# A packed attention with a gated MLP: the second product by seven products instead of eight, and float16 weights parked in DRAM

## The chip, the core and the metric

The kernel runs on one core of a Trainium2 chip. The metric is the time of one execution in device microseconds (us), and less is better. On the core, TensorE (PE in the profile) multiplies matrices into PSUM, a small accumulator memory; VectorE (DVE), ScalarE (ACT) and GpSimd (POOL) do elementwise work; SyncE (SP) only starts DMAs here. Each engine takes its instructions in the order in which the program lists them and waits on semaphores for the others. SBUF is the on-chip memory of 128 partitions in which tiles live; DRAM is the memory that DMAs read and write.

## What is computed

Eight batches of eight heads, 576 tokens and 64 values a head. 32 "packed" rows a head attend to the tokens, then the tokens attend to the packed rows; the result, 4608 tokens of 512 values, goes through an RMS norm and a gated MLP of width 1536.

```python
p_packed = sm_attn(p, k, v)                 # 32 rows a head
out = sm_attn(q, p_packed, p_packed)        # all tokens
x = out, heads side by side                 # 4608 x 512
xn = x / sqrt(mean(x * x) + 1e-06) * rms_g
g = xn @ w_gate                             # 512 -> 1536
val = xn @ w_val
return (g * sigmoid(g) * val) @ w_out       # 1536 -> 512
```

`sm_attn` is a softmax over scaled scores times the values. `q`, `k`, `v`, `p` and the output are float32; the MLP's weights arrive as 64-bit floats, and the kernel turns them into float32 first (`to_f32`, line 484).

## The kernel before

**The arithmetic.** The attention result of a token is its softmax weights over 8 x 32 = 256 packed rows times those rows. So gate and value can be taken straight from the 256 softmax weights, if the packed rows of each batch are first multiplied into `w_gate` and `w_val`. These are the *packed weights* (`packed_weights`, line 1184): per batch six chunks `c` of 256 gate and 256 value columns. The *first product* is then softmax weights (256 deep) times packed weights; its result passes through SiLU and the multiplication of gate and value; the *second product* multiplies the resulting `h` (1536 deep) by `w_out`. Most float32 values are held as a sum of two float16 parts, high and low, and a product is three float16 matmuls into one accumulator: high by high, high by low, low by high.

**The loops.** `mlp` (line 1590) goes over 12 units `u` of 384 tokens, which are three tiles of 128. For each of 12 blocks `ft` of 128 hidden columns it makes gate and value (line 1620: two depths of 128 and three passes, six matmuls of 384 columns each). A batch has 576 tokens, so units 1, 4, 7 and 10 hold tokens of two batches: there every matmul is split into two of 192 columns, since each batch has its own packed weights. `gated` (line 1660) then takes SiLU on ScalarE (line 1671), multiplies on VectorE (line 1674), and splits the result into high (line 1694, ScalarE) and low part (line 1700, VectorE, the difference of a float32 and a float16 tile in SBUF). After the 12 blocks, each of the three tiles runs 36 matmuls of 512 columns against `w_out` (line 1656), and `store` (line 1706) scales the result (line 1712) and sends it out (line 1715).

**Packed weights.** They live in a ring of eight places, six being one batch, so most chunks of batch b+1 can only be made while the unit at the boundary uses up the chunks of batch b (mark `used`). For batches 0 to 3 they are made from float32 weights (line 1212), for batches 4 to 7 (`PW16_FROM`) in three float16 passes (line 1223). In between `weights16` (line 1231) turns the weights in `wgv` in place into two float16 parts, through VectorE (line 1238), ScalarE (line 1240) and GpSimd (line 1242). `pw_evict` brings the packed weights from PSUM into the ring as high and low parts (`split`, lines 457 and 459).

**Everything else** runs beside this: `keysets` and `stage1` make the packed rows of the next batches, `query` (line 1326) loads and transposes the queries of a unit and `attention` (line 1394) makes its softmax weights; `query` may start when the first product of unit u - 2 has been issued (mark `po`). Many of the transposes are DMAs.

**The order.** All engines' instructions are written out by a small planner in the file (`Plan`, line 88). Each piece of work is a generator that yields its engine and an estimated cost. The planner picks the next piece by the earliest estimated start within a window (`CHOICE`) and a rank for each kind of work (`RANK`, `LATER`); `Room`s are buffers that are handed round, among them four PSUM banks `pm` that first product, second product and packed weights share, and two output buffers `o`. Strings such as `H_LO` say for each block which engine does an operation ("A" ScalarE, "D" VectorE, "P" GpSimd). The planner's times fix the order within each engine's queue, those of SP included; what runs when is then settled by semaphores.

## Time and profile before

| quantity | value |
|---|---|
| time, median of 3 runs | 779.63 us (779.62, 779.63, 781.18) |
| span of the profiled execution | 778.5 us; the fastest run is 1.1 us longer than it, which lies around the span |
| TensorE's granted clock, mean | 0.991 |
| bytes moved by DMA | 82.21 MB, 135509 packets |

The profile is one execution. Its page gives each engine's busy time, the chain of work that ended last and the costliest groups of instructions; further views answer for a stretch of time or a line. A group reads: line, engine, operation, written tile <- read tiles, shapes, count, then busy us and mean ns of one, then the idle time of the engine before it and who ended that. A row in order of time reads: start, duration, engine, line, operation, tiles, count, and in brackets idle time before it. Matmuls are pipelined, so a matmul's own duration is longer than the distance to the next one. PEld are weight loads, which overlap matmuls.

### The profile page before, as it was taken

The page shows a single profiled execution, that of the slowest core. Times are in us where ns is not written, and L with a number is a line of the kernel's source. Part 1 is how long each engine was busy: PE and PEld are TensorE (multiplying, and loading weights), DVE is VectorE, ACT ScalarE, POOL GpSimd, SP SyncE. Part 2 cuts the span into 40 slices and gives each one's busy share as a digit, 9 for nine tenths or more (in the row PEclk, how much of TensorE's full clock was granted, in tenths as well). Part 3 has the DMA queues.
Part 4 walks back from the last instruction along what each step waited for, and adds up shares of the span by engine and source line. Part 5 has one row for each costly group of instructions (what it writes and reads, how often), then busy time and mean ns, then how long its engine had stood idle before and what let it go on. Part 6 is the DMA issues. An engine that isn't in the chain of part 4 may idle for free.

```text
span 778.5 us, 18543 instructions
## 1 busy us (share of the span) xinstructions
PE 738.2 (95%) x7778; PEld 436.5 (56%) x7778; DVE 507.1 (65%) x1095; ACT 473.4 (61%) x910; POOL 84.3 (11%) x95
## 2 busy tenths in 40 slices
PE   8767899999999989999989999999999999999998
PEld 6533564686445455576544456468455455685553
DVE  1698889685585687589688559458468355472341
ACT  3679987676586668587678558447357265271230
POOL 1545121000000012013311000000000000000000
PEclk9899999999999999999999999999999999999999
DMA  9999700565366436636436653723213212300001
GB/s 255 386 278 259 232 16 21 99 114 143 72 114 145 86 66 153 140 66 139 107 85 116 104 136 63 160 66 62 55 49 63 68 35 64 92 19 26 27 1 41
DMA packets 135509, 82.21 MB, mean 106 GB/s; under 512 B 98433, under 2 KB 123009, under 8 KB 135425
## 3 DMA queue, kind: packets, MB, share of 16 engines
q1 hardware_dynamic: 135424, 81.02, 43.8%
q8 instruction: 61, 1.00, 0.5%
q14 instruction: 24, 0.19, 0.1%
HBM read 47.97 MB, written 9.44 MB: 74 GB/s over the span
## 4 chain that ended last, share of the span: by engine, by line
PE 72%; DVE 12%; DMA 6%; ACT 5%; issue 2%; SPq 1%; POOL 1%; DVEq 0%; ACTq 0%; POOLq 0%
PE pm_3x L1656 9%; PE pm_1x L1656 8%; PE pm_2x L1656 8%; PE pm_2x L1620 7%; PE pm_0x L1620 7%; PE pm_1x L1620 7%; PE pm_3x L1620 7%; PE pm_0x L1656 6%; DMA ring<-in_moe_w_gate_dram 2%; PE quad L1421 1%; PE quad L1058 1%; DVE ring L459 1%; PE quad L1498 1%; DMA big_5x<-in_v_dram 1%; DVE wgv L499 1%
## 5 line engine op out<-in xcount | busy, mean ns | idle before, releaser
L1620 PEld LDWEIGHTS <-ring 128*128 128x128 f16 x2304 | 204.8, 98 | 107.3 <-issue 36.6
L1656 PEld LDWEIGHTS <-hall 128*128 128x128 f16 x1296 | 123.6, 98 | 146.4 <-issue 8.4
L1656 PE MATMUL pm_2x<-wo,hall 128*128 128x512 f16 x360 | 81.9, 379 | 0.0
L1656 PE MATMUL pm_3x<-wo,hall 128*128 128x512 f16 x360 | 81.7, 379 | 0.0
L1656 PE MATMUL pm_1x<-wo,hall 128*128 128x512 f16 x324 | 74.8, 379 | 0.0
L1694 ACT CAST hall<-t_1x 128x384 f16<-128x384 f32 x71 | 36.3, 511 | 34.7 <-DVE t_1x L1674 34.6
L1656 PE MATMUL pm_0x<-wo,hall 128*128 128x512 f16 x252 | 56.9, 379 | 0.0
L1620 PE MATMUL pm_2x<-aTu_0x,ring 128*128 128x384 f16 (+1 forms) x312 | 45.8, 289 | 1.8 <-DVE ring L459 1.4
L1694 ACT CAST hall<-t_0x 128x384 f16<-128x384 f32 x70 | 35.5, 508 | 18.8 <-DVE t_0x L1674 18.7
L1700 DVE TENSOR_TENSOR hall<-t_1x,hall 128x384 f16<-128x384 f32 x70 | 39.7, 567 | 10.7 <-ACT hall L1694 9.1
L1620 PE MATMUL pm_2x<-aTu_1x,ring 128*128 128x192 f16 (+1 forms) x312 | 43.7, 283 | 1.3 <-ACT t_0x L1671 0.9
L1620 PE MATMUL pm_3x<-aTu_0x,ring 128*128 128x192 f16 (+1 forms) x312 | 42.4, 280 | 2.6 <-DVE ring L459 2.6
L1620 PE MATMUL pm_1x<-aTu_1x,ring 128*128 128x192 f16 (+1 forms) x300 | 42.3, 284 | 2.2 <-DVE o_1x L1712 1.2
L1700 DVE TENSOR_TENSOR hall<-t_0x,hall 128x384 f16<-128x384 f32 x70 | 40.0, 571 | 6.6 <-ACT hall L1694 6.4
L1620 PE MATMUL pm_0x<-aTu_1x,ring 128*128 128x192 f16 (+1 forms) x300 | 42.4, 285 | 0.0
L1620 PE MATMUL pm_0x<-aTu_0x,ring 128*128 128x384 f16 (+1 forms) x240 | 37.7, 298 | 2.1 <-ACT t_1x L1671 1.5
L1620 PE MATMUL pm_3x<-aTu_1x,ring 128*128 128x384 f16 (+1 forms) x240 | 36.6, 294 | 2.7 <-ACT t_1x L1671 1.9
L1620 PE MATMUL pm_1x<-aTu_0x,ring 128*128 128x192 f16 (+1 forms) x288 | 39.0, 279 | 0.1
L1532 POOL TENSOR_TENSOR trio_6x<-trio_5x,neghalf 128x3 f32<-128x3 f32 x6 | 5.1, 852 | 232.0 <-DVE trio_5x L1526 232.0
L1242 POOL TENSOR_TENSOR wgv<-o_0x,wgv 128x512 f16<-128x512 f32 x12 | 14.4, 1203 | 107.7 <-ACT wgv L1240 65.0
L1532 POOL TENSOR_TENSOR trio_2x<-trio_1x,neghalf 128x3 f32<-128x3 f32 x6 | 5.1, 856 | 152.1 <-DVE trio_1x L1526 152.0
L1454 ACT ACTIVATE hl_0x<-e_0x 128x768 f16<-128x768 f32 x10 | 8.4, 843 | 20.9 <-DVE e_0x L1445 15.6
(917 smaller groups left out, 1348.7 us busy)
## 6 DMA issues: line engine op xcount, KB each, us to landing
out_dram<-o_0x SPq DMA_DIRECT2D x18, 256.0 KB, 2.0
out_dram<-o_1x SPq DMA_DIRECT2D x18, 256.0 KB, 2.0
hall<-in_moe_w_out_dram SPq DMA_DIRECT2D x4, 1024.0 KB, 5.4
wo<-in_moe_w_gate_dram SPq DMA_DIRECT2D x3, 1024.0 KB, 15.5
wo<-in_moe_w_val_dram SPq DMA_DIRECT2D x3, 1024.0 KB, 11.5
big_5x<-in_v_dram SPq DMA_DIRECT2D x5, 576.0 KB, 6.7
big_0x<-in_v_dram SPq DMA_DIRECT2D x4, 576.0 KB, 6.6
big_3x<-in_k_dram SPq DMA_DIRECT2D x4, 576.0 KB, 6.5
```

Source lines behind the costliest of these rows:

```text
L459: nc.vector.scalar_tensor_tensor(lo, x, s, hi, ALU.mult, ALU.subtract)
L499: nc.vector.scalar_tensor_tensor(d, d, 3, lo, ALU.logical_shift_left, ALU.bitwise_or)
L1058: nc.tensor.matmul(pp[32 * j : 32 * j + 32, :D], a1T[:, c, 32 * j : 32 * j + 32], vf[:, j, cv, :], start=(c == 0), stop=(c == NCK - 1),)
L1242: nc.gpsimd.tensor_tensor(wgv16[:, c, k, 1], st, wgv16[:, c, k, 0], ALU.subtract)
L1421: nc.tensor.matmul(ps2[o : o + n, i, :, pi, :], qT[:, lq, i, pi, o : o + n], packs[b][3][:, lp, pi, :, :], start=(j == 0), stop=(j == 2),)
L1454: nc.scalar.activation(ehl[:, :, 0, :], e, AF.Copy, scale=2.0**14)
L1498: nc.tensor.matmul(px[o : o + n, j, i, g, :], aT[h, i, la, g, o : o + n], packs[b][2][g][h, lp, :], start=(n3 == 0), stop=(n3 == 2), tile_ ...
L1532: nc.gpsimd.tensor_tensor(ru, var, neghalf.broadcast_to([P, TPU]), ALU.pow)
L1620: nc.tensor.matmul(psi[:, :, o : o + n], pw[:, g, lw, w, f * P : (f + 1) * P], aT[:, :, la, g, o : o + n], start=(j == 0), stop=(j == 5),)
L1656: nc.tensor.matmul(po, hall[:, ft, lh, ts], wo[:, ft, 1 - lw, :], start=(n == 0), stop=(n == 3 * NFT - 1))
L1694: nc.scalar.copy(hall[:, ft, 0, :], t)
L1700: nc.vector.tensor_tensor(hall[:, ft, 1, :], t, hall[:, ft, 0, :], ALU.subtract)
```

## The change

1. From token 768 on (`GROUPS_FROM` = 2 units) the MLP goes by 15 groups `g` of 256 tokens (two tiles) instead of units of 384. The first product makes 2 x 128 hidden columns by 256 tokens in one PSUM bank, in matmuls of 256 columns; where the two tiles are of different batches, or a batch ends inside a tile, in pieces of 128 or 64 (`pieces`). For this the tokens of units 4, 7 and 10 are dealt to the tiles so that only the middle tile holds two batches (`blocks`); loads and stores follow. Attention, queries and keys still go by units of 384.
2. From group 7 on (`SEVEN_FROM`) the second product is done by Strassen's scheme. The 256 tokens by 256 hidden columns of a chunk are a 2 x 2 block matrix, the 256 hidden columns by 512 outputs another. Instead of eight products of 128 x 128 by 256 blocks there are seven, in which one or both factors are sums of blocks (`out_seven`). Four sums on the side of `h` are made by GpSimd for every chunk (`sums`) and split into float16 parts with `h` itself (`halves`): 7 blocks of 128 columns instead of 4. The four sums on the side of `w_out` are made once (`differences`). `collect` adds the seven products up into the two output tiles, with one ScalarE and seven VectorE operations of 256 columns in place of two of 512. Groups 3 to 6 keep the old form in the new tiling (`out_plain`).
3. The float16 weights are ready from batch 2 on (`PW16_FROM` 4 -> 2), so the conversion runs earlier. Each chunk's float16 parts are written once to DRAM (`keep`, 6 x 1 MB); from batch 3 on each chunk is brought back into one of three places of `wgv` before its packed weights are made (`bring`, 30 x 1 MB, at most three chunks ahead). The other three places then hold the sums of `w_out`.
4. The planner's constants, its ranks, the engine strings and some buffers are others; branches that no setting used are gone.

The core of the diff:

```diff
-SLACK = (0.317, 0.223)
-CHOICE = ({'pe': 0.1, 'act': 0.458, 'dve': 0.275, 'pool': 0.298, 'sp': 0.833}, {'pe': 0.0, 'act': 0.417, 'dve': 0.193, 'pool': 0.208, 'sp': 0.274})
+SLACK = (0.175, 0.244)
...
-PW16_FROM = 4
-V16_FROM = 8
+PW16_FROM = 2
...
+GROUPS_FROM = 2
+SEVEN_FROM = 7
+NGT = 256
+AHEAD = 4
+T_HI = "ADADAA"
+T_LO = "DDDPDD"
+G_HI = "AADAAA"
+G_LO = "DDDDDD"
+S_BY = "PPPP"
+S_HI = "AAAAAA"
+S_LO = "DPPDDD"
...
+    tb = wgv[:, :3].rearrange("p c k w f -> p (c k w f)").bitcast(F16)
+    tb = tb.rearrange("p (k c l n) -> p k c l n", k=4, c=NFC, l=2)
+    dram = ctx.enter_context(tc.tile_pool(name="dram", bufs=1, space=bass.MemoryType.DRAM))
+    kept = [dram.tile([P, NKT * 2 * 2 * P], F32, name=f"kept{c}") for c in range(NFC)]
...
+    seven = hall0.rearrange("p (c l k t) -> p c l k t", c=NFC, l=2, k=7)
...
+    aTus = cpool.tile([P, 2 * TPU, 2, 2, P], F16, name="aTus")
+    for i in range(2):
+        plan.rooms[f"aTu{i}"] = [(0.0, aTus[:, TPU * i : TPU * (i + 1)])]
+    plan.rooms["s"] = []
...
+            w16 = wgv16[:, c]
             if b == PW16_FROM:
                 yield ("wgv16", c, NKT - 1)
+            elif b > PW16_FROM:
+                yield ("brought", b, c)
+                w16 = wgv16[:, brought_at(b, c)]
...
+            if k == NKT - 1:
+                plan.add(keep(c), "keep", c)
+    def keep(c):
+        yield LOAD, P * 8192
+        nc.sync.dma_start(kept[c], wgv[:, c].rearrange("p k w f -> p (k w f)"))
+        plan.mark("kept", c)
+    def brought_at(b, c):
+        return 3 + (NFC * (b - PW16_FROM - 1) + c) % 3
+    def bring():
+        for n in range(NFC * (B - PW16_FROM - 1)):
+            b, c = PW16_FROM + 1 + n // NFC, n % NFC
+            if n < 3:
+                yield ("pw16", PW16_FROM, 3 + n)
+                yield ("kept", 3 + n)
+            else:
+                yield ("pw16", *divmod(n - 3 + NFC * (PW16_FROM + 1), NFC))
+            yield ("kept", c)
+            yield LOAD, P * 8192
+            nc.sync.dma_start(wgv[:, brought_at(b, c)].rearrange("p k w f -> p (k w f)"), kept[c])
+            plan.mark("brought", b, c)
+    def differences(c):
+        for i in range(3):
+            yield ("pw16", PW16_FROM, i)
+            yield ("kept", i)
+        yield ("wo_hl", c)
+        room = yield Room("big")
+        r = room[:, : 4 * NGT].rearrange("p (f n x) -> p f n x", f=2, n=2)
+        x = wo[:, 2 * c : 2 * c + 2].rearrange("p f l (n x) -> p l f n x", n=2)
+        yield POOL, pool(4 * NGT)
+        nc.gpsimd.tensor_tensor(r, x[:, 0], x[:, 1], ALU.add)
+        for to, a, b in (((0, 0), (0, 1), (0, 0)), ((0, 1), (1, 1), (0, 1)), ((1, 1), (1, 1), (0, 0)), ((1, 0), (1, 0), (1, 1))):
+            yield POOL, pool(NGT)
+            nc.gpsimd.tensor_tensor(r[:, *to], r[:, *a], r[:, *b], ALU.subtract)
+        rr = r.rearrange("p f n x -> p (f n) x")
+        if T_HI[c] == "A":
+            yield ACT, act(4 * NGT)
+            nc.scalar.copy(tb[:, :, c, 1], rr)
+        else:
+            yield DVE, 0.074 + 0.53e-3 * 4 * NGT
+            nc.vector.tensor_copy(tb[:, :, c, 1], rr)
+        if T_LO[c] == "D":
+            yield DVE, dve(4 * NGT)
+            nc.vector.tensor_tensor(tb[:, :, c, 0], rr, tb[:, :, c, 1], ALU.subtract)
+        else:
+            yield POOL, pool(4 * NGT)
+            nc.gpsimd.tensor_tensor(tb[:, :, c, 0], rr, tb[:, :, c, 1], ALU.subtract)
+        plan.give("big", room)
+        plan.mark("tb", c)
...
+    def blocks(u):
+        (b, r, _, n), *more = parts(u)
+        if not more or u < EARLY:
+            return [(b, 0, TPU, o, n, r) for b, r, o, n in parts(u)]
+        return [
+            (b, 0, 2, 0, n, r), (b, 0, 1, n, P - n, r + 2 * n),
+            (b + 1, 1, TPU, n, P - n, 0), (b + 1, 2, TPU, 0, n, 2 * (P - n)),
+        ]
...
+        ahead = TPU * u // 2 - AHEAD
+        if ahead >= GROUPS_FROM * TPU // 2:
+            yield ("po", ahead, "group")
+        elif u > 1:
+            yield ("po", min(u - 2, GROUPS_FROM - 1))
...
+        yield from by_units()
+        if SEVEN_FROM == GROUPS_FROM * TPU // 2:
+            plan.add(sums_rooms(), "sums")
+        for g in range(GROUPS_FROM * TPU // 2, NU * TPU // 2):
+            yield from group(g)
+    def by_units():
...
+    def pieces(g):
+        at = [tile_parts(*x) for x in group_tiles(g)]
+        if at[0] == at[1]:
+            return [(b, slice(0, 2), o, n) for b, o, n in at[0]]
+        return [(b, slice(i, i + 1), o, n) for i in range(2) for b, o, n in at[i]]
+    def group(g):
+        tiles = group_tiles(g)
+        us = sorted({u for u, _ in tiles})
+        n0 = TPU * (tiles[0][0] % 2) + tiles[0][1]
+        aT = aTus[:, n0 : n0 + 2]
+        later = {x[0] for n in range(2 * g + 2, TPU * NU) for x in tile_parts(*divmod(n, TPU))}
+        done_b = sorted({x[0] for x in pieces(g)} - later)
+        for u in us:
+            yield ("aTu", u)
+        for c in range(NFC):
+            for b in sorted({x[0] for x in pieces(g)}):
+                yield ("pw", b, c)
+            for u in us:
+                yield ("sc", u)
+            pss, done = [], []
+            for w in range(2):
+                ps = yield Room("pm")
+                psi = ps.rearrange("p (f i t) -> p f i t", f=2, i=2)
+                yield PE, pe(NGT, 12)
+                for f in range(2):
+                    for b, i, o, n in pieces(g):
+                        pw = ring[:, slot_of(b, c)]
+                        j = 0
+                        for k in range(2):
+                            for lw, la in ((0, 0), (0, 1), (1, 0)):
+                                nc.tensor.matmul(
+                                    psi[:, f, i, o : o + n], pw[:, k, lw, w, f * P : (f + 1) * P], aT[:, i, la, k, o : o + n],
+                                    start=(j == 0), stop=(j == 5),
+                                )
+                                j += 1
+                pss.append(ps)
+                done.append(plan.now)
...
+            plan.add(gated_pair(g, c, pss, done), "gated", g, c)
+            for b in done_b:
+                plan.mark("used", b, c)
...
+        plan.mark("po", g, "group")
+        if g < SEVEN_FROM:
+            yield from out_plain(g)
+        else:
+            yield from out_seven(g)
+        plan.mark("out", g)
...
+        yield SILU, sum(act(NGT * (b - a)) + 0.1 for a, b, _ in sides), done[0]
+        for a, b, u in sides:
+            nc.scalar.activation(tv[:, :, a:b], pg[:, :, a:b], AF.Silu, scale=units[u][0][:, c, 0:1])
+        plan.give("pm", pss[0])
+        yield DVE, sum(dve(NGT * (b - a)) + 0.1 for a, b, _ in sides), max(plan.now, done[1])
+        for a, b, u in sides:
+            nc.vector.scalar_tensor_tensor(tv[:, :, a:b], pv[:, :, a:b], units[u][0][:, c, 1:2], tv[:, :, a:b], ALU.mult, ALU.mult)
+        plan.give("pm", pss[1])
...
+        if g < SEVEN_FROM:
+            yield from halves(seven[:, c, :, 0:4], tk, G_HI[c], G_LO[c], 4)
+            plan.give("t", t)
+            plan.mark("h", g, c)
+            return
+        plan.add(sums(g, c, t, tk, t_t), "sums", g, c)
+        yield from halves(seven[:, c, :, 0:3], tk[:, 1:4], G_HI[c], G_LO[c], 3)
+        plan.mark("h", g, c)
+    def sums(g, c, t, tk, t_t):
+        s = yield Room("s")
+        sk = [s[:, k // 2, k % 2] for k in range(4)]
+        for n, (k, x, y, op) in enumerate((
+            (sk[0], tk[:, 0], tk[:, 2], ALU.add), (sk[2], tk[:, 1], tk[:, 0], ALU.subtract),
+            (sk[1], sk[0], tk[:, 1], ALU.subtract), (sk[3], tk[:, 3], sk[1], ALU.subtract),
+        )):
+            yield (POOL, pool(P), t_t) if S_BY[n] == "P" else (DVE, dve(P), t_t)
+            (nc.gpsimd if S_BY[n] == "P" else nc.vector).tensor_tensor(k, x, y, op)
+            t_t = plan.now
+        plan.add(done_with(g, c, t), "sums", g, c)
+        yield from halves(seven[:, c, :, 3:7].rearrange("p l (a b) t -> p l a b t", a=2), s, S_HI[c], S_LO[c], 4)
+        plan.give("s", s)
+        plan.mark("hs", g, c)
...
+    def out_seven(g):
+        b11, b21, b22 = (wo[:, f::2, :, n * NGT : (n + 1) * NGT] for f, n in ((0, 0), (1, 0), (1, 1)))
+        t1, t3, t4, t2 = (tb[:, k] for k in range(4))
+        terms = {1: (0, b11), 2: (2, b21), 3: (6, b22), 4: (1, t4), 5: (3, t1), 6: (4, t2), 7: (5, t3)}
+        def product(k, cs):
+            a, b = terms[k]
+            for c in cs:
+                yield ("h" if a < 3 else "hs", g, c)
+            yield PE, pe(NGT, 3 * len(cs))
+            for c in cs:
+                for n, (lh, lw) in enumerate(((0, 0), (0, 1), (1, 0))):
+                    nc.tensor.matmul(
+                        s[k][:, :NGT], seven[:, c, lh, a, :], b[:, c, 1 - lw, :],
+                        start=(c == 0 and n == 0), stop=(c == NFC - 1 and n == 2),
+                    )
+        yield "seven",
+        early, late = range(NFC - 1), range(NFC - 1, NFC)
+        banks[g] = s = {}
+        for k in (1, 2):
+            s[k] = yield Room("pm")
+            yield from product(k, early)
+        for k in (1, 2):
+            yield from product(k, late)
+            plan.mark("p", g, k)
...
+        for k in (6, 7, 5, 4, 3):
+            s[k] = yield Room("pm")
+            yield from product(k, range(NFC))
+            plan.mark("p", g, k)
...
+        def plus(to, k, by, last=True):
+            yield ("p", g, k)
+            yield DVE, dve(NGT) + 0.1
+            nc.vector.scalar_tensor_tensor(to, s[k][:, :NGT], invE, by, ALU.mult, ALU.add)
+            if last:
+                plan.give("pm", s[k])
+        yield ("p", g, 1)
+        yield ACT, act(NGT) + 0.1
+        nc.scalar.activation(ob[:, one], s[1][:, :NGT], AF.Copy, scale=invE)
+        plan.give("pm", s[1])
+        yield from plus(ob[:, two], 6, ob[:, one])
+        yield from plus(ob[:, one], 2, ob[:, one])
+        yield from plus(oa[:, one], 7, ob[:, two])
+        yield from plus(oa[:, two], 5, oa[:, one], False)
+        yield from plus(ob[:, two], 5, ob[:, two])
+        yield from plus(oa[:, one], 4, oa[:, one])
+        plan.add(send(ua, ia, oa), "store", ua, ia)
+        yield from plus(ob[:, two], 3, ob[:, two])
+        yield from send(ub, ib, ob)
```

448 lines of the change are left out of this document (188 added, 260 removed).

## The prediction

> **What bounds the kernel now.** I read the page first, then the busy time of each engine stage by stage, then the order of matmuls in time, then the costs of the single operations, and last the waits.
>
> ```profile
> span 778.5 us, 18543 instructions
> PE 738.2 (95%) x7778; PEld 436.5 (56%) x7778; DVE 507.1 (65%) x1095; ACT 473.4 (61%) x910; POOL 84.3 (11%) x95
> PE 72%; DVE 12%; DMA 6%; ACT 5%; issue 2%; SPq 1%; POOL 1%; DVEq 0%; ACTq 0%; POOLq 0%
> ```
>
> TensorE is busy 738.2 of 778.5 us and carries 72% of the chain that ended last. The stages (columns: stretch, its length, busy us of PE, PEld, DVE, ACT, POOL, clock, DMA share, GB/s) show where it is not:
>
> ```profile
> 0.00:80.00 80.00, 58.73 (x643) 38.82 (x644) 53.83 (x115) 54.01 (x88) 33.61 (x47) 0.91 0.98 297
> 80.00:160.00 80.00, 75.55 (x794) 46.11 (x794) 64.39 (x134) 63.46 (x113) 13.13 (x14) 1.00 0.36 84
> 160.00:340.00 180.00, 174.67 (x1930) 99.92 (x1927) 126.31 (x294) 121.82 (x245) 11.98 (x11) 1.00 0.53 113
> 340.00:420.00 80.00, 75.96 (x950) 46.87 (x935) 66.50 (x141) 61.89 (x126) 20.03 (x17) 1.00 0.45 95
> 420.00:640.00 220.00, 218.46 (x2445) 125.33 (x2444) 136.61 (x299) 124.09 (x248) 3.86 (x4) 1.00 0.40 84
> 640.00:760.00 120.00, 120.00 (x972) 72.93 (x970) 57.92 (x114) 48.14 (x97) 1.70 (x2) 1.00 0.15 37
> ```
>
> Of the idle 40 us, 25.7 lie before 160 us, while the weights arrive (DMA share 0.98). From 160 to 760 us TensorE idles 10.9 us, and the more the fuller VectorE is: 0.7% at DVE 62% (420 to 640), 3% at 70%, 5% at 83% (340 to 420, where the weights are turned into float16). The clock is full. So matmul time taken out after 160 us is time gained, as long as nobody else becomes late.
>
> **The matmuls, counted.** What one costs is the distance between starts:
>
> ```profile
> 682.18 1.16 PE L1620 MATMUL pm_2x<-aTu_0x,ring 128*128 128x192 f16 x12
> 683.18 1.15 PE L1620 MATMUL pm_3x<-aTu_0x,ring 128*128 128x192 f16 x12
> 684.17 1.15 PE L1620 MATMUL pm_1x<-aTu_0x,ring 128*128 128x192 f16 x12
> ```
> ```profile
> 727.93 1.14 PE L1620 MATMUL pm_1x<-aTu_1x,ring 128*128 128x384 f16 x6
> ...
> 751.33 1.89 PE L1656 MATMUL pm_1x<-wo,hall 128*128 128x512 f16 x8
> ```
> ```profile
> 759.27 7.77 PE pm_2x L1656 x36
> ```
> ```profile
> 142.44 1.22 PE L1421 MATMUL quad<-pbd,big_2x 128*128 128x64 f16 x36
> 143.50 2.75 PE L1656 MATMUL pm_1x<-wo,hall 128*128 128x512 f16 x12
> ```
>
> 512 columns: 7.77/36 = 215.8 ns. 384: (751.33-727.93)/144 = 162.5. That is 0.4164 ns a column and 2.6 ns a matmul; it gives 82.5 for 192 columns (row: 1.99/24 = 82.9) and 29.2 for 64 (row: 1.06/36 = 29.4, with new 128x128 weights each time). So 256 columns cost 109.2 and 128 cost 55.9.
>
> 1. Second product. A group of 256 tokens took 72 matmuls of 512: 15.54 us. Seven products of 6 chunks and 3 float16 passes are 126 of 256: 13.76. Eleven groups (7 to 17): 11 x 1.78 = 19.6 us less. This sits on the TensorE path.
> 2. First product. The columns stay, the pieces shrink: before 2304 matmuls; after 432 for units 0 and 1, 10 plain groups of 144, two of 288 (a batch boundary between their tiles) and three of 432 (a boundary inside a tile): 3744. 1440 more x 2.6 ns = 3.7 us more.
> 3. Packed weights of batches 2 and 3 in float16 instead of float32 passes:
>
> ```profile
> 338.33 1.15 PE L1620 MATMUL pm_0x<-aTu_0x,ring 128*128 128x192 f16 x12 [1.45 <-ACT t_1x L1671]
> ...
> 340.43 1.16 PE L1620 MATMUL pm_3x<-aTu_0x,ring 128*128 128x192 f16 x12
> ```
> ```profile
> 680.32 1.15 PE L1620 MATMUL pm_3x<-aTu_0x,ring 128*128 128x192 f16 x12
> ```
>
> Twelve of 192 end their share at +0.995; a float32 chunk stood from 339.32 to 340.43 (1.11), a float16 one from 681.32 to 682.18 (0.86). 12 chunks x 0.25 = 3.0 us less.
>
> Matmul sum: -19.6 + 3.7 - 3.0 = -18.9 us.
>
> A rule speaks against the short pieces: every matmul here has its own weight load, and a load is recorded with 98 ns.
>
> ```profile
> L1620 PEld LDWEIGHTS <-ring 128*128 128x128 f16 x2304 | 204.8, 98 | 107.3 <-issue 36.6
> ```
>
> If loads did not overlap each other, the 1008 pieces of 128 columns (two groups of 288, three of 144) and 864 of 64 would cost 98 ns each: 1008 x 0.042 + 864 x 0.069 = 102 us more. The row of 64 columns at 29.4 ns, each with its load, says that they do overlap. [...]
>
> **The other engines.** Their prices:
>
> ```profile
> L1674 DVE SCALAR_TENSOR_TENSOR t_1x<-pm_1x,usc_1x,t_1x 128x384 f32<-128x384 f32 x16 | 9.9, 616 | 8.0 <-PE pm_1x L1620 4.2 <-ACT hall L1694 2.7 <-ACT t_1x L1671 1.0
> L1456 DVE SCALAR_TENSOR_TENSOR hl_0x<-e_0x,hl_0x 128x768 f16<-128x768 f32 x10 | 9.5, 950 | 1.6 <-ACT hl_0x L1454 1.6
> L459 DVE SCALAR_TENSOR_TENSOR hl_0x<-e_0x,trio_7x,hl_0x 128x256 f16<-128x256 f32 x15 | 7.0, 477 | 0.0
> L1712 DVE TENSOR_SCALAR o_1x<-pm_3x,invE 128x512 f32<-128x512 f32 x6 | 4.5, 750 | 13.6 <-PE pm_3x L1656 13.6
> ```
> ```profile
> L1240 ACT CAST wgv<-o_0x 128x512 f16<-128x512 f32 x12 | 7.3, 610 | 0.2 <-DVE o_0x L1238 0.2
> ```
> ```profile
> L1697 POOL TENSOR_TENSOR hall<-t_0x,hall x2: 912/914/915, 97.0 to 115.2; 128x384 f16<-128x384 f32 x2
> ```
> ```profile
> L1242 POOL TENSOR_TENSOR wgv<-o_0x,wgv x12: 1154/1160/1565, 273.2 to 415.6; 128x512 f16<-128x512 f32 x12
> ```
>
> VectorE by 0.92 ns a column: 0.48 at 256, 0.59 at 384, 0.71 at 512; GpSimd by 1.92: 0.42 at 128. Before, 256 tokens cost VectorE 8 x (0.62 + 0.59) + 2 x 0.75 = 11.2 us. A Strassen group costs 6 x 0.73 (product of gate and value) + 6 x 0.59 + 4 x 0.71 (remainders) + 7 x 0.48 (collecting) = 14.1: 2.9 more in about 33 us, so 62 to 70% becomes 71 to 79%. GpSimd, nearly idle, gets 24 x 0.42 + 2 x 1.16 = 12.4 us a group. That alone fits in time, but the two exclude each other:
>
> ```profile
> 384.35 0.28 DVE L459 SCALAR_TENSOR_TENSOR pd_0x<-pf_0x,tiny_67x,pd_0x 128x64 f16<-128x64 f32 x1 [0.41 <-ACT pd_0x L457]
> ...
> 384.90 1.17 POOL L1242 TENSOR_TENSOR wgv<-o_1x,wgv 128x512 f16<-128x512 f32 x1 [1.40 <-ACT wgv L1240]
> ...
> 385.11 1.04 DVE L459 SCALAR_TENSOR_TENSOR pd_0x<-pf_0x,tiny_67x,pd_0x 128x64 f16<-128x64 f32 x1 [0.47 <-ACT pd_0x L457]
> ```
> ```profile
> 415.55 1.56 POOL L1242 TENSOR_TENSOR wgv<-o_0x,wgv 128x512 f16<-128x512 f32 x1 [2.46 <-ACT wgv L1240]
> 415.55 0.54 DVE L1700 TENSOR_TENSOR hall<-t_0x,hall 128x384 f16<-128x384 f32 x1
> ```
>
> The same VectorE form with two inputs in SBUF takes 0.28 us, and 1.04 when GpSimd started just before it: it ends when GpSimd does. In the other order GpSimd takes 0.40 longer than its 1.16. So the sums on GpSimd and the remainders on VectorE (`halves`, x minus its float16 part, both in SBUF) take turns. In a Strassen group the turns begin when chunk 0 is gated (2.62 + 0.73 = 3.4 us) and must end when TensorE needs the sums of chunk 5: after the first product (15.7), products 1 and 2 (36 matmuls, 3.9) and 15 of product 6 (1.6), at 21.3. In 17.9 us go 12.4 of GpSimd and 6.4 of remainders, 18.8: 0.9 late, with ScalarE's 0.6 on the last chunk at most 1.5; and not late at all where the start of one operation overlaps the end of the one before it. I take the middle, 0.7 a group, 8 us in all, bounds 0 and 1.5 x 11 = 16.
>
> Other edits at no cost, with their cover. The float16 conversion moves from 273-416 us (the row of L1242) to beside unit 1 and groups 3 and 4: the 4.0 us of idling at 340-420 may move with it, plus or minus 4. The differences of the output weights (6 x (2.1 + 4 x 0.66), about 29 us of GpSimd by its 1.92 ns a column) have three groups of 15.7 + 15.5 us, 94 us, between batch 2's packed weights and group 7; late, they hold TensorE at "seven". The first 160 us keep their loads; other orders there are worth plus or minus 4. The last store is an operation of 256 instead of 512 columns, -0.3, left out.
>
> DRAM traffic: 6 writes and 30 reads of 1 MB.
>
> ```profile
> hall<-in_moe_w_out_dram SPq DMA_DIRECT2D x4, 1024.0 KB, 5.4
> wo<-in_moe_w_gate_dram SPq DMA_DIRECT2D x3, 1024.0 KB, 15.5
> ```
> ```profile
> SPq L1715 <- DVE o_0x L1712: 141.2, 11, 35.2
> ```
>
> At the 297 GB/s of the first stage 37.7 MB take 127 us, spread over the 480 us from 160 to 640 with a share of 0.40 to 0.53: room for it. Five of six pieces of a batch can come long before; the sixth waits for chunk 2 at the boundary and has three chunks and two weights (3 x 2.7 + 2 x 0.86 = 9.8 us) against 5.4 us to land; late, it holds TensorE's queue, with all behind it. The waits for a free piece stand in SP's queue ahead of q loads, transposes and stores, which already stand 141 us behind stores without stopping TensorE.
>
> Span: 778.5 - 18.9 + 8 = 767.6. The median of the runs stands 1.1 us above the span: **768.7 us**.
>
> **Rivals.**
> - Slower: the turns at SBUF set the pace. If ScalarE's 0.6 and attention's two-input operations (3 x 0.48 + 0.95 a unit, 1.6 a group) fall into the same window, seven groups are 0.9 + 0.6 + 1.6 = 3.1 us late and the four without attention beside them 1.5: 27.7 us, so 788. It turns the sign from 1.7 us a group on (18.9/11). For it: the rows above, and VectorE at 83% already costing 5%. Against: attention can go into the second product, where VectorE has 3.4 us of work in 13.8. [...] 0.13.
> - Brought weights late: landing in 15.5 us as in the loaded first stage, 5.7 us late in each of five batches: 797. Against: share 0.4 to 0.5 there. 0.03.
> - Weight loads set the pace of the short pieces: 102 us, 871. The 29.4 ns row is against. 0.02.
> - Better: the new order hides the turns and takes some of the 25.7 us at the start: 756 to 760. 0.13.
> - The gain eaten to within the noise: 0.03.
>
> **How the numbers follow.** The forecast (0 to 16 us of lateness: 760 to 777) has 0.66. About 0.2%, 1.6 us, is what a measurement can tell from no change. Faster 0.66 + 0.13 = 0.79, same 0.03, slower 0.18. The range is 757 to 783: it leaves out half of the better case and most of the slower ones, some 0.16.
>
> **What would show it.** Right: second-product matmuls 109 ns apart at 256 columns, 1386 of them; GpSimd about 84 + 136 + 29 = 250 us busy; TensorE idle after 160 us about 19 us, at the sixth product's sums. Wrong: gaps of over 1.7 us in each Strassen group; waits of the packed weights on their DMA; idle before 160 us changed by over 4 us.

## The result, and the profile after

The changed kernel takes 809.0 us (median of four runs, 805.4 to 811.7) against 779.6 us: 1.037 times as long, 95% interval 1.034 to 1.040. It is slower where the prediction said faster by 11 us. Two executions that ran far longer than the others of their kernel, one of 1492 us in the run e2_plain below (the one that was profiled) and one of 949 us of the kernel before, are left out of every ratio.

The profiled execution, the fastest of the four, took 805.4 us, 1.8 of them around its span. First the page of the changed kernel: span, busy time of each engine, and the shares of the chain that ended last.

```profile
span 803.6 us, 22901 instructions
...
PE 733.2 (91%) x9673; PEld 554.2 (69%) x9673; DVE 595.4 (74%) x1218; ACT 512.7 (64%) x959; POOL 290.3 (36%) x401
...
PE 49%; DVE 20%; POOL 10%; ACT 9%; issue 6%; DMA 3%; SPq 2%; POOLq 0%; DVEq 0%; ACTq 0%
```

TensorE's share of the chain falls from 72 to 49%, VectorE's rises from 12 to 20%, GpSimd's from 1 to 10%. The busy time of the same stages as before (columns as in the prediction):

```profile
0.00:80.00 80.00, 58.65 (x618) 40.11 (x618) 52.25 (x122) 51.21 (x78) 18.64 (x33) 0.87 0.93 283
80.00:160.00 80.00, 69.22 (x686) 38.55 (x683) 71.27 (x143) 60.37 (x108) 20.95 (x20) 1.00 0.35 103
160.00:340.00 180.00, 167.47 (x2035) 112.56 (x2033) 140.93 (x281) 128.91 (x244) 67.71 (x55) 0.98 0.65 161
340.00:420.00 80.00, 74.88 (x1233) 54.07 (x1232) 58.47 (x125) 55.36 (x107) 17.62 (x26) 0.98 0.76 190
420.00:640.00 220.00, 205.70 (x3064) 171.55 (x3062) 172.03 (x372) 145.07 (x286) 87.35 (x140) 0.99 0.63 150
640.00:760.00 120.00, 118.10 (x1703) 103.64 (x1701) 80.85 (x148) 60.63 (x120) 62.36 (x102) 1.00 0.30 93
```

TensorE now idles in every stage: 32.1 us before 160 (25.7 before), 12.5 from 160 to 340, 14.3 from 420 to 640 (1.5 before). VectorE is at 78% in both of the long stages. The matmuls themselves keep the predicted pace. This is the second product of a late group in order of time:

```profile
725.48 1.80 PE L1781 MATMUL pm_0x<-wo,hall 128*128 128x256 f16 x15
...
739.23 1.47 PE L1658 MATMUL pm_1x<-aTus,ring 128*128 128x256 f16 x12
```

126 matmuls of 256 columns in 13.75 us, 109.1 ns each, as the prediction had it.

The best place to cut the time in two is the first matmul of unit 1 (token 384). Three rows, of the kernel before, of the changed one, and of a run that is explained below:

```profile
148.03 0.66 PE L1620 MATMUL pm_2x<-aTu_1x,ring 128*128 128x192 f16 x6
```
```profile
158.62 0.58 PE L1593 MATMUL pm_3x<-aTus,ring 128*128 128x192 f16 x5
```
```profile
160.09 0.66 PE L1593 MATMUL pm_3x<-aTus,ring 128*128 128x192 f16 x6
```

So 10.6 us are lost before unit 1 begins. From there to the end the kernel before takes 630.5 us, the changed one 645.0: 14.5 more, where the matmul sum promised 18.9 less.

### The profile page after: what moved, and what is told of

It is laid out like the page before. It is cut to its first block, busy times and chain, and to the rows that moved or that the text cites. A ratio compares the mean times of both kernels' runs of the same rounds, so it can differ in the third digit from the quotient of the medians.

```text
span 803.6 us, 22901 instructions
## 1 busy us (share of the span) xinstructions
PE 733.2 (91%) x9673; PEld 554.2 (69%) x9673; DVE 595.4 (74%) x1218; ACT 512.7 (64%) x959; POOL 290.3 (36%) x401
## 3 DMA queue, kind: packets, MB, share of 16 engines
q8 instruction: 75, 1.23, 0.6%
## 4 chain that ended last, share of the span: by engine, by line
PE 49%; DVE 20%; POOL 10%; ACT 9%; issue 6%; DMA 3%; SPq 2%; POOLq 0%; DVEq 0%; ACTq 0%
POOL wo L1716 7%; PE pm_1x L1658 5%; PE pm_3x L1658 4%; PE pm_2x L1658 4%; PE pm_3x L1781 4%; PE pm_0x L1751 4%; PE pm_0x L1781 4%; PE pm_2x L1781 3%; PE pm_0x L1658 3%; PE pm_1x L1781 3%; DVE hall L1736 3%; PE pm_1x L1751 2%; DMA ring<-in_moe_w_val_dram 2%; DVE t_1x L1690 2%; DVE ring L468 2%
## 5 line engine op out<-in xcount | busy, mean ns | idle before, releaser
L1658 PEld LDWEIGHTS <-ring 128*128 128x128 f16 x3312 | 224.6, 98 | 37.6 <-issue 18.4
L1781 PEld LDWEIGHTS <-hall 128*128 128x128 f16 x1386 | 133.1, 98 | 29.8 <-DVE hall L1736 6.9
L1716 POOL TENSOR_TENSOR wo<-t_0x 128x128 f32<-128x128 f32 x66 | 37.9, 591 | 207.2 <-DVE t_0x L1690 207.2
L1658 PE MATMUL pm_2x<-aTus,ring 128*128 128x256 f16 (+2 forms) x840 | 70.0, 238 | 1.2 <-ACT t_0x L1686 1.1
L1658 PE MATMUL pm_1x<-aTus,ring 128*128 128x256 f16 (+2 forms) x816 | 69.5, 240 | 0.0
L1658 PE MATMUL pm_3x<-aTus,ring 128*128 128x256 f16 (+2 forms) x888 | 68.1, 232 | 0.9 <-issue 0.4
L1658 PE MATMUL pm_0x<-aTus,ring 128*128 128x256 f16 (+2 forms) x768 | 63.1, 236 | 4.7 <-issue 2.5
L1730 ACT CAST hall<-wo 128x512 f16<-128x512 f32 x66 | 40.7, 617 | 41.6 <-POOL wo L1716 41.2
L1751 PEld LDWEIGHTS <-hall 128*128 128x128 f16 x288 | 27.7, 99 | 33.4 <-issue 2.7
L1716 POOL TENSOR_TENSOR wo<-t_1x 128x128 f32<-128x128 f32 x66 | 40.9, 637 | 22.5 <-DVE t_1x L1690 22.5
L1593 PEld LDWEIGHTS <-ring 128*128 128x128 f16 x432 | 37.4, 98 | 16.4 <-issue 8.1
L1736 DVE TENSOR_TENSOR hall<-wo,hall 128x512 f16<-128x512 f32 x44 | 34.1, 777 | 14.9 <-ACT hall L1730 14.8
L1618 PEld LDWEIGHTS <-hall 128*128 128x128 f16 x216 | 20.5, 99 | 25.4 <-issue 3.6
L1781 PE MATMUL pm_2x<-wgv,hall 128*128 128x256 f16 x288 | 35.0, 273 | 1.2 <-DVE hall L1736 1.0
L1751 PE MATMUL pm_0x<-wo,hall 128*128 128x512 f16 x144 | 33.5, 385 | 0.0
L1781 PE MATMUL pm_1x<-wo,hall 128*128 128x256 f16 x198 | 25.5, 273 | 3.6 <-DVE hall L1736 2.0
```

The lines of the kernel that those rows point to most:

```text
L1593: nc.tensor.matmul(psi[:, :, o : o + n], pw[:, g, lw, w, f * P : (f + 1) * P], aT[:, :, la, g, o : o + n], start=(j == 0), stop=(j == 5),)
L1618: nc.tensor.matmul(po, hall[:, ft, lh, ts], wo[:, ft, 1 - lw, :], start=(n == 0), stop=(n == 3 * NFT - 1))
L1658: nc.tensor.matmul(psi[:, f, i, o : o + n], pw[:, k, lw, w, f * P : (f + 1) * P], aT[:, i, la, k, o : o + n], start=(j == 0), stop=(j == 5),)
L1716: (nc.gpsimd if S_BY[n] == "P" else nc.vector).tensor_tensor(k, x, y, op)
L1730: nc.scalar.copy(to[:, 0], x)
L1736: nc.vector.tensor_tensor(to[:, 1], x, to[:, 0], ALU.subtract)
```

## The experiments

In four of the runs (marked "same order") the planner still counts the work that is left out, so that every engine's queue keeps the order of the changed kernel word for word and only the named instructions are gone. "Rest" is the time from unit 1's first matmul to the end of the profile's span. It comes from one profiled execution of each run; e2_plain has no entry. Ratios are to the kernel before on the same chip, with their 95% intervals.

| run | median us | ratio | rest us |
|---|---|---|---|
| kernel before | 779.6 | 1 | 630.5 |
| changed kernel | 809.0 | 1.037 (1.034 to 1.040) | 645.0 |
| e1_before_order | 829.9 | 1.064 (1.060 to 1.067) | 683.3 |
| e2_plain | 805.6 | 1.032 (1.031 to 1.034) | |
| e3_plain_resident | 814.0 | 1.042 (1.040 to 1.045) | 651.8 |
| e4_no_sums | 792.4 | 1.015 (1.011 to 1.019) | 632.9 |
| e5_start_before | 800.5 | 1.026 (1.024 to 1.027) | 648.4 |
| e6_sums_out, same order | 795.7 | 1.021 (1.017 to 1.024) | 633.7 |
| e7_differences_out, same order | 801.6 | 1.028 (1.026 to 1.030) | 636.8 |
| e8_copies_out, same order | 801.3 | 1.027 (1.025 to 1.028) | 638.8 |
| e9_three_out, same order | 776.2 | 0.993 (0.992 to 0.995) | 613.6 |
| e10_sums_on_vector | 817.5 | 1.047 (1.044 to 1.049) | 654.7 |
| e11_late | 802.1 | 1.026 (1.024 to 1.029) | 653.6 |
| e12_late_units | 800.4 | 1.025 (1.022 to 1.027) | 651.3 |
| e13_last_two | 780.1 | 0.999 (0.998 to 1.000) | 631.3 |
| e14_last_three | 807.3 | 1.034 (1.032 to 1.035) | 658.4 |
| e15_last_none | 780.4 | 1.000 (0.999 to 1.001) | 632.3 |

**The order's numbers.** `SLACK`, `CHOICE`, `LATER`, `AGE`, the shared keys of `RANK` and the engine strings get the values of before:

```diff
-SLACK = (0.175, 0.244)
+SLACK = (0.317, 0.223)
...
-LOW = "DPPPPPPPDDPP"
+LOW = "PPPPPPPPPDPP"
```

> The changed kernel with the order of the kernel before: SLACK, CHOICE, LATER, AGE, the old keys of RANK and the engine strings have the numbers of before; tiling, Strassen and DRAM traffic stay. Theory A (the other order of the start costs most: token 768 is reached at 225.4 us instead of 211.1): token 768 comes at 211 to 215 us and the time falls by 10 to 14 us, to about 797. Theory B (GpSimd and VectorE taking turns at SBUF in the Strassen groups cost it): the start may move, the time stays within 3 us of 809, since the sums stay. Theory C (the trips to DRAM cost it): 809 as well.

Measured: 830, no theory's number. The start did return (unit 1 begins at 148.75 us, token 768 at 214.18), but the rest took 38 us longer. As a whole, the numbers that suited the old work do not suit the new. So only the first stage's values were put back (`SLACK = (0.317, 0.244)` and so on):

> Only what orders the work up to the attention of unit 1 (the first value of SLACK, CHOICE, AGE and RANK, LATER, and the engine strings of that stretch) gets the numbers of before; the second stage keeps the changed ones. Theory A, as mended by the first runs (the start costs about 11 us of the changed kernel's loss, and the second stage's numbers are right for the new work): token 768 at 214 us and the time at 796 to 800. Rival D (the planner's order is so touchy that any edit loses what it gains): token 768 at 214 us, but the time stays at 805 to 815.

Measured 800.5, 8.5 us less than the changed kernel; theory A expected 796 to 800, with token 768 at 214. Token 768, the first matmul after unit 1, is reached here at 219.4 us, against 225.35 in the changed kernel (up to 227.8 in the runs that keep its order) and 211.08 before:

```profile
211.08 0.81 PE L1620 MATMUL pm_3x<-aTu_0x,ring 128*128 128x384 f16 x4
```
```profile
225.35 0.71 PE L1658 MATMUL pm_3x<-aTus,ring 128*128 128x256 f16 x5
```
```profile
219.44 0.71 PE L1658 MATMUL pm_0x<-aTus,ring 128*128 128x256 f16 x5
```

Of the 14.3 us, 5.9 come back with the order; 8.4 do not. The run e11 below, which also moves the float16 conversion away from unit 1, gets there at 211.79:

```profile
211.79 0.60 PE L1658 MATMUL pm_0x<-aTus,ring 128*128 128x256 f16 x4
```

So in this order the other 7.7 us hang on the conversion, and on the first packed weights that follow it, beside unit 1. (The two runs also differ in where Strassen starts, but that lies far behind token 768.) The split is not fixed: e1 has the early conversion too, with 17 of its 24 pieces on GpSimd started before token 768 against 23 in e5, and gets there at 214.18. In the changed kernel itself 10.6 of the 14.3 us are lost before unit 1 and 3.7 beside it. Of the 10.6, e5 gets 8.4 back (its unit 1 begins at 150.24 us). Why the changed order of the start is slower was not followed further.

**Without Strassen.** Two runs have the old second product throughout (`SEVEN_FROM = 18`) and no differences; the second of them has no copies either.

> The second product is never Strassen's (SEVEN_FROM 18) and the differences of the output weights are left out, since nothing reads them; groups of 256 tokens, early float16 and DRAM traffic stay. The matmuls become 19.6 us longer. Theory A: the waits at line 1781 (about 10 us) and the wait of batch 3's packed weights beside the differences (about 8 us) go, so 809 + 19.6 - 18 = 811. Theory B: all 44 us lost go with the sums: 809 + 19.6 - 44 = 785. Theory C: 809 + 19.6 = 829, less what the differences cost.

> As the run before, and without the DRAM copies: the float16 weights stay in their six places (no differences need room), nothing is written out or brought back. Theory C: faster than the run with the traffic by 10 us or more, since packed weights wait for their pieces. Theories A and B: within 3 us of it, since the pieces of 1 MB land in about 6 us and the packed weights' waits name ScalarE and VectorE.

Measured 805.6 and 814.0. The first lies between theory A's 811 and theory B's 785: taken as it stands, Strassen with its sums and differences costs some 3 us more than the 19.6 us that it saves. But the order moved here. The second is worse than the first, although it has less to do. Without the copies the planner arranged the conversion otherwise, and in that order the first product of unit 1 alone took 42.7 us instead of 35.0. An experiment that lets the order move carries differences of this size, 8 us in this stretch. This is why the next ones hold it fixed.

**The sums of h.** First with the planner free (the blocks of `h` are split in place of their sums):

> Leaves out the four sums of h on GpSimd in every Strassen group (the blocks of h themselves are split and multiplied in their place, so the output is another); matmuls, remainders, collecting and differences stay. Theory B: almost all of the loss goes: 765 to 772. Theory A: only the waits at line 1781 go, about 10 us, and perhaps 5 more of VectorE's slowed operations: 794 to 799.

Then in the same order:

```diff
-            (nc.gpsimd if S_BY[n] == "P" else nc.vector).tensor_tensor(k, x, y, op)
+            if g == SEVEN_FROM: (nc.gpsimd if S_BY[n] == "P" else nc.vector).tensor_tensor(k, x, y, op)
```

> The order on every engine is kept word for word; the four sums of h on GpSimd are left out in ten of the eleven Strassen groups (old sums are split and multiplied in their place, so the output is another). Theory A: the sums' own lateness is the 10.6 us that TensorE idles inside the second products plus about 5 us of slower evictions, so 793 to 797. Theory B (all of the loss is the turns at SBUF): below 775. If only the waits inside the second products go: 800.

Measured 792.4 and 795.7. The second is in theory A's range, the first 2 us below it, and theory B's numbers are far off. In the same order the rest is 11.3 us shorter for ten groups without sums, 1.1 a group. The remainders on VectorE from 415 to 800 us, by tile (columns: count, shortest, median and longest in ns, first and last start), show how, first in the changed kernel, then without the sums:

```profile
L1736 DVE TENSOR_TENSOR hall<-t_0x,hall x31: 544/747/1524, 417.3 to 785.9; 128x384 f16<-128x384 f32 x31
L1736 DVE TENSOR_TENSOR hall<-t_1x,hall x31: 542/804/853, 420.0 to 787.9; 128x384 f16<-128x384 f32 x31
```
```profile
L1736 DVE TENSOR_TENSOR hall<-t_0x,hall x31: 545/557/809, 417.3 to 774.5; 128x384 f16<-128x384 f32 x31
L1736 DVE TENSOR_TENSOR hall<-t_1x,hall x31: 544/557/805, 419.9 to 776.9; 128x384 f16<-128x384 f32 x31
```

The same instruction takes 557 ns without GpSimd beside it and 750 to 800 with it. That fits the turn-taking that the prediction read from its rows (0.28 us alone, 1.04 when GpSimd had just started). TensorE's waits inside the second products (L1781), for `h` and for its sums, are 6.8 us in the changed kernel and 1.7 without the sums. The largest of the changed kernel (columns: us in all, times, longest):

```profile
PE pm_1x L1781 <- DVE hall L1736: 2.0, 3, 0.9
PE pm_2x L1781 <- DVE hall L1736: 1.7, 4, 0.7
PE pm_1x L1781 <- ACT hall L1730: 1.6, 3, 1.0
```

The 11.3 us are the price of the sums as a whole. How much of it is the turns, and how much the time that the sums themselves take on GpSimd before they can be split, is not separated.

The sums were then given to VectorE (`S_BY = "DDDD"`, `S_LO = "DDDDDD"`):

> The four sums of h and all remainders of the sums go to VectorE (S_BY DDDD, S_LO DDDDDD), so that GpSimd has nothing in a Strassen group and no turns at SBUF are left. If the turns are the sums' price: 801 to 806, though VectorE gets 24 short sums a group more. If VectorE's room is the price (it is 71 to 79% busy in those stages): 812 or more.

Measured 817.5, 8.4 us slower. From 415 to 800 us VectorE is busy 306.7 us there against 275.3. In this run doing the sums on VectorE costs more than taking turns, as the second expectation said (812 or more if VectorE has no room). The order moved here, so part of the 8.4 us may be the order's.

**The differences of the output weights**, left out in the same order:

> Same order; all instructions of the differences of the output weights are left out (the products read what lies in that place, so the output is another). If their 2.6 to 3.1 us turns at SBUF hold up batch 3's packed weights (TensorE idles 5.7 us and loses 10 us against its pace between 286 and 313 us): 798 to 802. Rival: that wait has another cause (the packed rows of batch 3 come late on their own): within 2 us of 809.

Measured 801.6; the rest is 8.2 us shorter. The stretch in order of time, first in the changed kernel:

```profile
283.85 2.95 DVE L1204 TENSOR_TENSOR wgv<-big_3x,wgv 128x1024 f16<-128x1024 f32 x1
...
285.68 3.10 POOL L1191 TENSOR_TENSOR big_1x<-wo 128x1024 f32<-128x1024 f16 x1
...
287.50 2.36 DVE L1204 TENSOR_TENSOR wgv<-big_0x,wgv 128x1024 f16<-128x1024 f32 x1
...
289.78 0.14 DVE L450 TENSOR_SCALAR uv<-quad 128x1 uint32<-128x1 uint32 x1
...
290.41 2.56 POOL L1191 TENSOR_TENSOR big_3x<-wo 128x1024 f32<-128x1024 f16 x1
...
291.82 2.03 DVE L1053 TENSOR_TENSOR pbd<-pts_0x,pbd 64x128 f16<-64x128 f32 x2
...
293.86 0.72 DVE L1061 TENSOR_TENSOR pg_1x<-pts_0x,gcol 128x128 f32<-128x128 f32 x1
...
294.62 0.31 ACT L466 ACTIVATE pgh_1x<-pg_1x 128x128 f16<-128x128 f32 x1 [2.19 <-DVE pg_1x L1061]
...
294.98 0.39 PE L1132 MATMUL pm_2x<-wgv,pgh_1x 64*32 64x512 f16 x1 [4.78 <-ACT pgh_1x L466]
```

and without the differences:

```profile
286.23 0.16 DVE L450 TENSOR_SCALAR uv<-quad 128x1 uint32<-128x1 uint32 x1 [1.29 <-PE quad L1022]
...
288.51 0.57 DVE L1053 TENSOR_TENSOR pbd<-pts_0x,pbd 64x128 f16<-64x128 f32 x2
...
289.10 0.29 DVE L1061 TENSOR_TENSOR pg_1x<-pts_0x,gcol 128x128 f32<-128x128 f32 x1
...
291.37 0.39 PE L1132 MATMUL pm_2x<-wgv,pgh_1x 64*32 64x512 f16 x1
```

The packed rows of batch 3 pass through VectorE (L450, L1053, L1061) on their way to TensorE. With the differences, a remainder of 1024 columns (L1204, 2.4 and 3.0 us) stands ahead of them in VectorE's queue, and their own two operations (L1053) take 2.03 us instead of 0.57 while GpSimd works (the L1191 that starts at 290.41 runs until 292.97). TensorE has the packed weights next in its queue and waits 4.8 us.

**The DRAM copies**, left out in the same order:

> Same order; the DMAs that write the float16 weights to DRAM and bring them back are left out (packed weights are made from whatever stands in the three places, so the output is another). Theory C (copies late): 795 or less. Theory A: within 3 us of 809, since no wait of the packed weights ends with a DMA.

Measured 801.3, between the two theories; the rest is 6.2 us shorter. The expectation that nobody waits for the copies held: in the changed kernel no wait of the packed weights ends with one. The loss is elsewhere. TensorE's waits from 348 to 380 us in the changed kernel, and from 349 to 378 us without the copies:

```profile
PE pm_0x L1658 <- issue: 2.5, 1, 2.5
PE pm_3x L1132 <- issue: 1.0, 1, 1.0
```
```profile
PE pm_2x L1132 <- issue: 0.7, 1, 0.7
PE quad L1518 <- DVE tiny_48x L910: 0.4, 1, 0.4
```

"issue" is waiting for nothing that the profile shows. Without the copies the longer wait is gone, and 0.7 us are left at the packed weights (L1132); the section on the hardware comes back to the longer one. Another 1.9 us wait, for a load of `v` at 592.8 us, is gone as well, but it is only 0.4 us in the run without the sums, which has the copies.

**All three at once**, same order:

> The three leavings-out at once, in the changed kernel's own order: no sums of h after the first Strassen group, no differences of the output weights, no DRAM copies (the output is another). Alone they were worth 11.3 us (sums), 8.4 us (differences) and 6.3 us (copies) of TensorE's pace from 158 us on. Theory A (they add up, each at its own place): 783, and what is then left over the kernel before less 18.9 us of matmuls, some 20 us, lies in the first 225 us and in waits of the new order. Rival (they hide one another): 788 to 795.

Measured 776.2 where theory A expected 783, faster than the kernel before by 0.5 to 0.8%. The rest is 31.4 us shorter than in the changed kernel, where the three alone sum to 25.7 (by the medians 32.8 and 28.5). That they do not hide one another is shown. The busy times from unit 1 on, before, changed, and with the three left out, close the account:

```profile
148.00:778.50 630.50, 614.93 (x6477) 360.29 (x6475) 398.96 (x864) 364.93 (x726) 37.56 (x34) 1.00 0.39 84
```
```profile
158.60:803.60 645.00, 606.73 (x8391) 476.90 (x8389) 473.26 (x957) 401.15 (x775) 250.72 (x348) 0.99 0.55 139
```
```profile
160.00:773.70 613.70, 597.65 (x8392) 476.14 (x8389) 436.34 (x950) 395.37 (x771) 77.30 (x77) 1.00 0.42 86
```

With the three out, TensorE's busy time is 17.3 us below that of before, and its idle time is the same, 16.1 against 15.6. So of the predicted matmul gain of 18.9 us 17.3 are there. In the changed kernel 22.2 us more idle time and 9.1 us more busy time for the same matmuls lie on top of it. The idle time adds up: the three runs alone take out 8.6 (sums), 8.0 (differences) and 5.5 us (copies), some 22. The busy time does not: alone they take out 2.8, 0.3 and 0.7 us. So nearly all of the 5.7 us that the three give more together is busy time; the section on the hardware shows how much of it is the clock.

**Other placings.** Two runs have Strassen in the last six groups only, the conversion where it was (`PW16_FROM = 4`), and the first stage's old numbers; the second also keeps units of 384 up to token 3072 (`GROUPS_FROM = 8`).

> The order up to unit 1's attention from before, float16 weights from batch 4 as before (PW16_FROM 4: conversion where it was, 18 pieces brought instead of 30), Strassen in the last six groups only (SEVEN_FROM 12). From 809: start and conversion beside unit 1 -13, the longer matmuls of five groups +8.9, no sums where attention is beside them -8, differences in another place -5, fewer copies -3: 789. Rival D (a new order loses by itself): 795 to 805.

> As the run before, and tiled by units of 384 tokens up to token 3072 (GROUPS_FROM 8), so that only the six Strassen groups have the short pieces: 2 to 3 us less than it, 786. Against the kernel before this leaves 6 x 1.78 = 10.7 us less of matmuls against sums, differences and copies: if those cost under 10 us in this place, it beats 780.

Measured 802.1 and 800.4: the start is right, but both lose where the differences now stand. In e12 the first product of unit 5, which runs beside them, takes 46.9 us, with 12.1 of idle time, where the kernel before needs 33.5; in e11 TensorE idles 11.7 us from 420 to 480. The rival's 795 to 805 was right for e11, and the 786 expected of e12 was not.

Three last runs have everything in the order of before, no copies, units up to token 3840 (`GROUPS_FROM = 10`, `PW16_FROM = 4`), and the differences only when the last packed weights are made:

```diff
-SEVEN_FROM = 7
+SEVEN_FROM = 16
...
-            yield ("pw16", PW16_FROM, i)
-            yield ("kept", i)
+            yield ("pw16", B - 1, i)
```

> Order and float16 weights as in the kernel before (PW16_FROM 4, nothing written to DRAM), units of 384 up to token 3840, then three groups of 256, the last two of them by Strassen; the differences of the output weights wait until batch 7's packed weights are made, about 690 us, and have 55 us to group 16. Against before: 2 x 1.78 less, 288 x 2.6 ns = 0.75 more for pieces, and 0.45 idle in each as in the changed kernel's last groups: 1.9 us less, ratio 0.9975. Rival D (every new order loses): ratio 1.005 or more.

> The same with three Strassen groups. The differences (about 25 us of GpSimd, with VectorE and ScalarE for the halves) have only the first product of group 15, from about 690 to 702 us, before TensorE needs them at the fifth product. If GpSimd is as slow as in the changed kernel (2.6 us an operation of 1024): 10 to 15 us late, ratio 1.01 to 1.02. If they fit: ratio 0.996.

> The control: the last three groups by 256 tokens with the old second product, no differences, no sums. Theory: 0.75 us more than before for the shorter pieces, ratio 1.001, at most 1.002. Rival: the grouping itself costs more (SiLU and product of four blocks at once come later): 1.003 or more.

Measured 0.9993, 1.034 and 0.9998. The control (e15) says that the grouping costs nothing at the end. Against it, two Strassen groups with nothing else beside them gain 0.9 us in the profile (15.0 and 14.8 us for second products of 15.5 and 15.7, and 0.5 given back in a first product) of the 3.6 that the matmuls promise; the ratio to the kernel before (0.998 to 1.000) tells neither from no change, and leaves out the 0.9975 that was expected. With three groups the differences come later than expected, and hold TensorE at another place:

```profile
PE pm_3x L1652 <- ACT t_1x L1680: 24.4, 1, 24.4
```

This is the first product of group 15. By the program, sums need buffers that become free only with the differences; until then neither `t` buffer is handed back, SiLU cannot start, and TensorE stands. No version here that does all the work is measurably faster than the kernel before.

## Why the prediction was wrong

- **The matmul sum (-18.9) was right.** 109 ns a matmul, 1386 of them, and 17.3 us less busy time once the three parts are out.
- **The step that failed is "Other edits at no cost, with their cover", together with the copies' "room for it".** The differences were checked against GpSimd's room and the copies against the DMA engines' share, and each had room there. Neither was checked against what stands behind it in VectorE's queue, or beside it in time. The differences had 94 us of cover and cost 8.2; the copies cost 6.2; the start, entered as nothing with plus or minus 4, cost 10.6. That is 25 us from terms entered as zero, of the 36 that lie between the forecast span of 767.6 us and the measured 803.6. The others are 3.3 of the sums (11.3 for 8), the 5.7 that the three cost only together, and 2.1 from matmuls and idle time.
- **The conversion's term (plus or minus 4) held.** Beside unit 1 it cost 3.7 us, but they come back later: with the three parts out, TensorE idles from unit 1 on as long as before (16.1 and 15.6 us).
- **The turns at SBUF (0.7 a group, bounds 0 and 1.5):** the sums with their turns cost 1.1 a group, inside the bounds, and the remainders are slower beside GpSimd (medians of 747 and 804 ns, against 557 without the sums). The place was mostly wrong. Of the 6.8 us that TensorE waited inside the second products, 1.2 were at the sixth product's sums. The others were in the first two, for the last parts of `h` itself, which stand behind the others.
- **The rivals.** The slower one put 28 us on the turns alone; the sums with their turns cost about 12. What happened is a case that was not on the list: several delays, among them some on VectorE, which had been filled from 65 to 74%. The edits with bounds of plus or minus 4 were entered as zero, as if they could go either way; the start, the differences and the copies all went one way. That VectorE is what the first two have in common is argued; the copies do not load it. Brought weights that come late were rightly held unlikely. So were weight loads as the pace: 36 matmuls, 12 of 128 columns and 24 of 64, took 1.37 us at 724 us, and the prediction's prices give 1.38.
- **Its own signs.** Idle time before 160 us changed by 6.4 us, over the 4 that it named as a sign of being wrong. TensorE idled 38.3 us after 160 us instead of 19, and GpSimd was busy 290 us instead of 250. Gaps of over 1.7 us in every Strassen group, or packed weights waiting for their DMA, did not appear.

## What to carry to other kernels

Work that is moved to an idle engine need not be free: on GpSimd, busy 11% of the time before, the sums cost 11.3 us here and the differences 8.2. Look at what it shares with the engine that feeds the bottleneck: at what stands behind it in that queue, and at what else runs at the place where it lands. Several edits that all load one engine may well err in the same direction; then their bounds add. To price a part of a change, leave its instructions out while the order of all the others is held fixed, for new planner numbers alone moved this kernel by 8.5 us one way (e5) and 21 the other (e1).

## What the runs showed of the hardware

**Three gaps cost more than their length.** After the 4.8 us wait at 290 us the granted clock (the third column from the right) is 0.57 for the next 8 us; after the 2.45 us wait at 360 us it is 0.60 for 4 us. The third row is the stretch of the first without the differences, where TensorE does not wait:

```profile
295.00:303.00 8.00, 7.11 (x103) 3.29 (x104) 7.81 (x16) 2.31 (x7) 6.13 (x9) 0.57 0.57 196
```
```profile
363.00:367.00 4.00, 4.00 (x78) 3.00 (x84) 2.69 (x7) 0.69 (x1) 0.85 (x1) 0.60 1.09 247
```
```profile
295.00:303.00 8.00, 8.00 (x46) 3.64 (x39) 7.27 (x16) 4.58 (x9) 0.00 (x0) 1.00 0.99 320
```

The first gap so costs about 3.4 us more (8 x 0.43). Added up over slices of 4 us from unit 1 on, the clock below full takes 6.8 us in the changed kernel, 6.8, 7.3 and 7.1 in the runs without sums, differences or copies, and 1.7 with all three out. So about 5 of the 9.1 us of longer busy time above are the clock, which the prediction did not price, and leaving out one part alone does not lower it; the other 4 stay open. In slices of one us the clock reads 0.50 in both stretches; at that reading it was low for some 3.2 us after the second gap (4 x 0.40 / 0.5) and 6.9 after the first (8 x 0.43 / 0.5). Nearly all that is left of the changed kernel's 6.8 us lies behind a third wait, of 2.80 us, which ends at 459.3 us: the clock from 459 to 463 us is 0.57. After TensorE's other waits from unit 1 on, the longest of 1.89 us, it reads 1.00.

**TensorE may have waited for its own instructions.** The 2.45 us "issue" wait falls into a run of 36 matmuls of one chunk, 26 of which had run:

```profile
359.19 1.25 PE L1658 MATMUL pm_0x<-aTus,ring 128*128 128x128 f16 x26
...
362.90 0.45 PE L1658 MATMUL pm_0x<-aTus,ring 128*128 128x64 f16 x10 [2.45 <-issue]
```

The DMA queues from 359 to 364 us (packets, MB, share of the engines) are full, and one packet of instructions passes among 677 others:

```profile
q1 hardware_dynamic: 677, 1.83, 100.6%
q8 instruction: 1, 0.02, 1.2%
```

On the page of the profile that queue has 75 packets and 1.23 MB, 61 and 1.00 before. That is 16 KB a packet, and 258 of TensorE's 19346 matmuls and weight loads for each (before 15556, 255 for each; in e2_plain 18158 and 71 packets, 256 for each). In these three kernels the packets grow with TensorE's instructions. This wait, 2.1 to 2.7 us long, is in the changed kernel and in the runs without sums, without differences and with the sums on VectorE, which all keep the copies; it is in neither of the two same-order runs that leave them out. That this queue brings TensorE's instructions, and that the copies delayed them, is argued from these numbers, not shown by itself; with all three parts out, other "issue" waits of 1.3 and 1.0 us stand though no copy runs.
